# A gated linear attention in front of a two-level mixture of experts: scans with a PSUM operand, scores by row halves, compact state, small first units

## The chip, the cores and the metric

The kernel runs on one core of one Trainium2 chip. The metric is the device time of one execution in microseconds (us). Three runs of the kernel before took 591.95 us in the median (591.56 to 595.39).

## The reference

Two parts follow each other. The attention part has 4 batches, 8 heads, 768 time steps and head size 48; per head it carries a 48 x 48 state:

```
for t in range(S):
    state = alpha[:, :, t, :, None] * state + einsum('bhd,bhe->bhde', k[:, :, t], v[:, :, t])
    y[:, :, t] = einsum('bhd,bhde->bhe', q[:, :, t], state)
```

Its output, 3072 rows of 384, goes through a mixture of 16 experts in 4 groups: each row takes the best group, then the best expert of it, both by the largest logit; its row of the output is `combined * (relu(x @ w1[g, e]) @ w2[g, e])` with w1 of 384 x 1024, w2 of 1024 x 384 and `combined` the product of the two softmax weights. All data is float32.

## The kernel before, in words

**Attention.** The 768 steps of a batch are cut into 6 chunks of 128, so there are 24 chunks, numbered n = 0 to 23, and one turn of the main loop (line 385) per chunk; it is called a step below. Heads are taken in pairs p = 0 to 3: one head of a pair lies on partitions 0 to 47, the other on 64 to 111, so R = 112 partitions are used. Within a chunk the decay is turned into weights on q and k, so that the chunk's inner sum is a masked matrix product, and a state is carried from chunk to chunk.

- `decayed(u, p)` (lines 164 to 191) prepares one pair for a *unit* of 3 chunks (8 units). VectorE (DVE) runs a scan backward over 384 columns (`rev`, line 181), a reciprocal (line 184), a scan forward (`cq`, line 185) and the decay of the whole chunk (`tot`, line 187). GpSimd (POOL) multiplies k by `rev` (`kp`, line 188) and q by `cq` (`qp`, line 189). ScalarE (ACT) copies q into `qb` (line 191), where the two heads of a pair stand in separate columns with zeros between. Both scans multiply by the decay and add a tile (`ends`, `starts`) that lies in SBUF.
- `scores(n)` (line 193): 4 matmuls of 256 columns over all 112 rows into two PSUM banks (line 200); DVE masks each bank (`sm`, line 204).
- `outputs(n)` (line 237): 4 matmuls with the state (line 244), 8 with `v` (line 249), an ACT copy to `yt` (line 253).
- `next_state` (line 210): 4 transposes of `kp` (line 218), ACT copy to `kt` (line 219), 4 matmuls with `v` (line 224); DVE adds (line 230) and multiplies by `tot` (line 232), each once per head of the pair, into a state tile with zeros off the blocks.
- `to_rows` (line 256): 4 matmuls with `wr` (line 265), a DVE sum into logits (line 268), an ACT copy into the rows `x` (line 271).
- Once per batch `choose` (line 274, some two dozen short DVE operations) finds the expert, and `send` (line 330) counts places and writes the rows into `slots_d` in DRAM by indirect DMA from POOL (line 353). The last batch does this in three cuts.

**Experts.** For each of 16 experts the first 224 slots are fetched, transposed, and multiplied by w1 (line 443) and w2 (line 452); DVE scales and POOL scatters the rows of the output (line 457). A loop for slots beyond 224 follows (line 535).

**What sets the order.** Each engine runs its own instructions in order. A scheduler arranges them from the program text and from the buffers: tiles named in a pool rotate through its `bufs`, and an instruction that needs a buffer waits until its last reader is done. Loads of q, k and alpha (`qka`, 5 buffers) and of weights go through SyncE's (SP's) queue, `v` and `xg` through ACT's. The rows `x` of a batch have 2 buffers, so those of batch b wait for the indirect DMAs of batch b - 2 (the first write into them is line 323).

## Time and profile before

| | |
|---|---|
| median of 3 runs | 591.95 us |
| the profiled execution | 591.61 us, its span 589.9 us |
| TensorE busy | 492.1 us (83%) |
| VectorE busy | 225.6 us (38%) |
| GpSimd busy | 138.2 us (23%) |
| ScalarE busy | 105.0 us (18%) |
| DMA | 92.82 MB, mean 157 GB/s |

The span runs from the first to the last instruction; 1.7 us of the execution lie outside it. Busy shares are means over very unlike stages: the attention ends at about 235 us, and the experts take the rest. A step is located here by its matmuls with the state (line 244), which come once per n. [...] Each matmul of float32 appears as two records.

### The profile page before, as it was taken

The numbers are of one execution on the slowest core, as the hardware profiler recorded it, in microseconds if no ns is written. First come the engines' busy times: TensorE is split into PE (matmuls) and PEld (weight loads), VectorE is DVE, ScalarE is ACT, GpSimd is POOL, SyncE is SP. The second block draws the span as 40 slices with busy tenths as digits, with TensorE's granted clock in tenths as the row PEclk, the third lists the DMA queues.
The fourth block names the chain that finished last, engine by engine and source line by source line (L and its number), as shares of the span: only waits on it lengthen the run. The fifth ranks groups of instructions, "written<-read, shape, count | busy, mean of one in ns | idle before, by whom it ended". The sixth has DMA issues, their size and how long they took to land. (4 is left out here: it accounts for less than half of the span.)

```text
span 589.9 us, 6890 instructions
## 1 busy us (share of the span) xinstructions
PE 492.1 (83%) x2588; PEld 389.0 (66%) x2588; DVE 225.6 (38%) x607; ACT 105.0 (18%) x209; POOL 138.2 (23%) x141
## 2 busy tenths in 40 slices
PE   0475896786876798169999999999999999999992
PEld 0363785675765677166886688678767876887681
DVE  7748978768875775821111110111011101110100
ACT  0313333223232422100110111011101100110010
POOL 6506551456065503300011001100110010011001
PEclk9996797898789999559999999999999999999997
DMA  8983479444332002233645464555545554645000
GB/s 274 366 261 107 136 264 314 148 138 122 114 106 82 0 2 82 80 96 121 246 151 202 177 234 163 174 204 204 191 144 220 182 220 137 230 140 213 21 8 24
DMA packets 18674, 92.82 MB, mean 157 GB/s; under 512 B 2693, under 2 KB 6394, under 8 KB 14032
## 3 DMA queue, kind: packets, MB, share of 16 engines
q1 hardware_dynamic: 10512, 72.44, 35.7%
q10 hardware_dynamic: 4800, 10.46, 5.5%
q0 software_dynamic: 3328, 9.47, 4.3%
q8 instruction: 21, 0.34, 0.2%
q14 instruction: 13, 0.11, 0.1%
HBM read 77.36 MB, written 15.78 MB: 158 GB/s over the span
## 5 line engine op out<-in xcount | busy, mean ns | idle before, releaser
L452 PE MATMUL bank<-w,hT 128*96 128x384 f32 (+1 forms) x512 | 168.2, 487 | 0.0
L443 PEld LDWEIGHTS bank<-xt_e,w 128*128 128x128 f32 x768 | 147.6, 193 | 5.8 <-issue 2.4
L443 PE MATMUL bank<-xt_e,w 128*128 128x224 f32 x768 | 151.0, 357 | 0.6 <-DVE xt_e L432 0.6
L452 PEld LDWEIGHTS bank<-w,hT 128*96 128x96 f32 (+1 forms) x512 | 89.2, 177 | 70.1 <-issue 38.3
L457 POOL DMA_INDIRECT out_dram<-yo,dst x32 | 30.4, 950 | 301.2 <-DVE yo L455 274.6
L445 ACT ACTIVATE hT<-bank 128x448 f32<-128x448 f32 x64 | 34.8, 543 | 290.4 <-PE bank L443 290.4
L200 PE MATMUL bank<-qb,kp 112*128 112x256 f32 x192 | 58.4, 453 | 30.7 <-ACT qb L191 29.3
L455 DVE TENSOR_SCALAR yo<-bank,xg 128x384 f32<-128x384 f32 (+1 forms) x32 | 19.7, 615 | 154.1 <-PE bank L452 154.1
L200 PEld LDWEIGHTS bank<-qb,kp 112*128 112x128 f32 x192 | 41.9, 233 | 39.6 <-issue 18.2
L189 POOL TENSOR_TENSOR qp<-qka,cq 112x384 f32<-112x384 f32 x32 | 42.3, 1331 | 50.0 <-PE bank L244 33.0
L188 POOL TENSOR_TENSOR kp<-qka,rev 112x384 f32<-112x384 f32 x32 | 37.3, 1178 | 45.1 <-DVE rev L181 17.3
L224 PE MATMUL bank<-v,kt 128*112 128x96 f32 x160 | 22.9, 292 | 28.3 <-ACT kt L219 28.3
L191 ACT COPY qb<-qp 48x384 f32<-48x384 f32 x64 | 32.6, 510 | 64.6 <-POOL qp L189 63.9
L224 PEld LDWEIGHTS bank<-v,kt 128*112 128x112 f32 x160 | 19.3, 196 | 32.6 <-ACT kt L219 32.6
L485 DVE TENSOR_TENSOR dst<-xg,drop 128x1 int32<-128x1 f32 (+1 forms) x32 | 3.8, 155 | 95.1 <-DMA xg<-slots_d 54.5
L185 DVE TENSOR_TENSOR_SCAN cq<-qka,starts 112x384 f32<-112x384 f32 x32 | 39.7, 1244 | 0.5
L181 DVE TENSOR_TENSOR_SCAN rev<-qka,ends 112x384 f32<-112x384 f32 x32 | 33.7, 1059 | 10.8 <-POOL kp L188 6.4
L244 PE MATMUL bank<-qp,state 112*112 112x128 f32 x192 | 27.6, 291 | 11.6 <-DVE state L232 11.6
L244 PEld LDWEIGHTS bank<-qp,state 112*112 112x112 f32 x192 | 25.8, 191 | 15.7 <-issue 10.8
L204 DVE TENSOR_TENSOR sm<-bank,causal 128x512 f32<-128x512 f32 x48 | 32.0, 680 | 7.3 <-PE bank L200 7.0
L353 POOL DMA_INDIRECT slots_d<-x,place x24 | 23.6, 984 | 46.1 <-ACT yt L253 23.3
L265 PE MATMUL bank<-wr,yt 112*128 112x116 f32 x192 | 31.4, 316 | 0.0
(99 smaller groups left out, 290.2 us busy)
## 6 DMA issues: line engine op xcount, KB each, us to landing
w<-in_w_dram SPq DMA_DIRECT2D x32, 1536.0 KB, 6.8
qka<-in_qka_dram SPq DMA_DIRECT2D x32, 505.8 KB, 4.6
slots_d<-blank SPq DMA_DIRECT2D x1, 5404.0 KB, 28.2
v<-in_v_dram ACTq DMA_DIRECT2D x4, 1152.0 KB, 10.8
xg<-slots_d ACTq DMA_DIRECT2D x16, 193.0 KB, 6.7
xg<-slots_d ACTq DMA_DIRECT2D x16, 144.8 KB, 6.5
out_dram<-yo,dst POOLq DMA_INDIRECT x32, 6.0
slots_d<-x,place POOLq DMA_INDIRECT x24, 2.7
```

Source lines behind the costliest of these rows:

```text
L181: nc.vector.tensor_tensor_scan(out=flat(rev)[:, ::-1], data0=az[:, US:0:-1], data1=flat(ends)[:, ::-1], initial=0.0, op0=ALU.mult, op1=ALU ...
L185: nc.vector.tensor_tensor_scan(out=flat(cq), data0=az[:, 0:US], data1=flat(st), initial=0.0, op0=ALU.mult, op1=ALU.add)
L188: nc.gpsimd.tensor_tensor(out=flat(kp[:, p]), in0=k, in1=flat(rev), op=ALU.mult)
L189: nc.gpsimd.tensor_tensor(out=flat(qp[:, p]), in0=q, in1=flat(cq), op=ALU.mult)
L191: nc.scalar.copy(out=qd[r, p, :, i, :], in_=qp[r, p])
L200: nc.tensor.matmul(z[:, (p - g) * 2 * P:(p - g + 1) * 2 * P], lhsT=kp[:, p, c, :], rhs=qd[:, p, c].rearrange("r h s -> r (h s)"), start=Tr ...
L204: nc.vector.tensor_tensor(out=sm[:, 2 * g:2 * g + 4, :], in0=z.rearrange("p (h i) -> p h i", h=4), in1=causal[:, None, :].to_broadcast([P, ...
L224: nc.tensor.matmul(z[0:R, p * D2:(p + 1) * D2], lhsT=kt[:, p * R:(p + 1) * R], rhs=v[:, bc, p * D2:(p + 1) * D2], start=True, stop=True)
L244: nc.tensor.matmul(z[0:R, p * P:(p + 1) * P], lhsT=st[:, p, :], rhs=qp[:, p, c, :], start=(p == 0), stop=False, skip_group_check=True)
L443: nc.tensor.matmul(z[:, k * n:(k + 1) * n], lhsT=w1[:, dc, f * P:(f + 1) * P], rhs=xt[:, dc, 0:n], start=(dc == 0), stop=(dc == DC - 1))
L445: nc.scalar.activation(out=hT[:, f0:f0 + 2, 0:n], in_=z[:, 0:2 * n].rearrange("p (f t) -> p f t", f=2), func=AF.Relu)
L452: nc.tensor.matmul(zy[0:n, 0:DM], lhsT=hT[:, f, c0:c0 + n], rhs=w2[:, f, :], start=(f == 0), stop=(f == FC - 1))
```

## The change

Only the attention part and its input layout change; the experts' code is the same.

- **Scans.** Their second source lies in PSUM: one bank `starts`, filled with 3e38, with one column of ones. A chunk has 129 columns, the first of them a decay of 3e38; the scans multiply and take the minimum, so that at this column they restart at the second source. The backward scan's first column of each chunk is then the chunk's whole decay, and `tot` goes away. PSUM is left with 7 banks for the rest in place of 8.
- **Scores.** Per pair two matmuls of 128 columns, one over partitions 0 to 47 and one over 64 to 111, each into the bank of its head. `qb` and its ACT copies go away.
- **State.** It is kept compact (112 x 4 x 48); the matmuls with `v` write each head into its own half (8 matmuls of 48 columns), DVE does two adds and one multiply, and ACT copies it into tiles with zeros off the blocks (`blocks`). The transposes come before `outputs`.
- **Order.** Units are 1, 2 and then 7 times 3 chunks (9 units). Decays, `choose` and `send` are cut into portions that a queue `later` hands out at three places of a step. The rows `x` have 3 buffers, the loads 8, each in two DMAs. The blanking of `slots_d`, the weights' loads and the loads of `qka` stand later in a step.

```diff
@@ the pools
-    xp = ctx.enter_context(tc.tile_pool(name="xrows", bufs=2))
+    xp = ctx.enter_context(tc.tile_pool(name="xrows", bufs=3))
-    pp = ctx.enter_context(tc.tile_pool(name="psum", bufs=8, space=PSUM))
+    pp = ctx.enter_context(tc.tile_pool(name="psum", bufs=7, space=PSUM))
...
-        inp = gla.enter_context(tc.tile_pool(name="inp", bufs=5))
+        inp = gla.enter_context(tc.tile_pool(name="inp", bufs=8))
...
+        fix = gla.enter_context(tc.tile_pool(name="fix", bufs=1, space=PSUM))
+        starts = fix.tile([P, 512], F32, name="starts")
+        one_col = starts[0:R, 511:512]
+        nc.vector.memset(starts, HUGE)
+        nc.vector.memset(one_col, 1.0)
...
+        units = [(0, 0, 1), (0, 1, 2), (0, UC, UC)]
+        units += [(b, c, UC) for b in range(1, B) for c in (0, UC)]
@@ decayed
-            nc.vector.tensor_tensor_scan(out=flat(rev)[:, ::-1], data0=az[:, US:0:-1],
-                                         data1=flat(ends)[:, ::-1], initial=0.0,
-                                         op0=ALU.mult, op1=ALU.add)
-            nc.vector.reciprocal(out=st[:, :, 0], in_=rev[:, :, 0])
-            nc.vector.tensor_tensor_scan(out=flat(cq), data0=az[:, 0:US], data1=flat(st),
-                                         initial=0.0, op0=ALU.mult, op1=ALU.add)
-            nc.vector.tensor_tensor(out=tot[:, :, p], in0=rev[:, :, 0], in1=a0, op=ALU.mult)
-            nc.gpsimd.tensor_tensor(out=flat(kp[:, p]), in0=k, in1=flat(rev), op=ALU.mult)
-            nc.gpsimd.tensor_tensor(out=flat(qp[:, p]), in0=q, in1=flat(cq), op=ALU.mult)
-            for i, r in enumerate(heads):
-                nc.scalar.copy(out=qd[r, p, :, i, :], in_=qp[r, p])
+            def back():
+                nc.vector.tensor_tensor_scan(
+                    out=flat(rev)[:, ::-1], data0=a[:, W:0:-1],
+                    data1=one_col.to_broadcast([R, W]), initial=1.0, op0=ALU.mult, op1=ALU.min)
+                nc.gpsimd.tensor_tensor(out=kp, in0=k, in1=rev[:, :, 1:A1], op=ALU.mult)
+
+            def forth():
+                nc.vector.reciprocal(out=st.rearrange("r (c s) -> r c s", s=A1)[:, :, 0],
+                                     in_=rev[:, :, 0])
+                nc.vector.tensor_tensor_scan(out=flat(cq), data0=a[:, 0:W], data1=st, initial=1.0,
+                                             op0=ALU.mult, op1=ALU.min)
+                nc.gpsimd.tensor_tensor(out=qp, in0=q, in1=cq[:, :, 1:A1], op=ALU.mult)
+
+            return [(1.0, back), (1.2, forth)]
@@ scores
+            z = [bank() for _ in heads]
+            for p in range(HP):
+                for i, r in enumerate(heads):
+                    nc.tensor.matmul(z[i][:, p * P:(p + 1) * P], lhsT=kp[r, p, c, :],
+                                     rhs=qp[r, p, c, :], start=True, stop=True)
+            for i in range(2):
+                nc.vector.tensor_tensor(out=sm[:, i], in0=z[i].rearrange("p (h i) -> p h i", h=HP),
+                                        in1=causal[:, None, :].to_broadcast([P, HP, P]),
                                         op=ALU.mult)
...
@@ next_state
+            for p in range(HP):
+                for i, r in enumerate(heads):
+                    h = 2 * p + i
+                    nc.tensor.matmul(z[r, p * D:(p + 1) * D],
+                                     lhsT=kt[:, p * R + r.start:p * R + r.stop],
+                                     rhs=vs[b][:, bc, h * D:(h + 1) * D], start=(p == 0), stop=True,
+                                     skip_group_check=True)
...
+                for r in heads:
+                    nc.vector.tensor_tensor(out=new[r], in0=old[r], in1=add[r], op=ALU.add)
+                nc.vector.tensor_tensor(out=new, in0=new, in1=tot.to_broadcast([R, HP, D]),
+                                        op=ALU.mult)
+            blk = blocks[1 + n % 2]
+            for r in heads:
+                nc.scalar.copy(out=blk[r, :, r], in_=new[r])
@@ the main loop
+            if c == 0 and u + 1 < NU:
+                make(u + 1)
+            if n + 1 < LAST and where[n + 1][1] == 0:
+                spend(1e9)
+            sm_next = scores(n + 1) if n + 1 < LAST else None
+            carry = (n + 1) % NC and n + 1 < LAST
+            kt = turned_keys(n) if carry else None
+            spend(2.0)
+            yt_next = outputs(n, sm, blk)
+            if n + 1 < LAST:
+                blk = next_state(n + 1, kt) if carry else blocks[0]
+            spend(1.2)
+            if yt is not None:
+                send_chosen()
+                rows_and_choice(n - 1, yt)
+            spend(1.2)
```

On TensorE one step in the middle of the program (scores, state matmuls, `v` matmuls, transposes, state update, rows) stands before as:

```order
L200 MATMUL bank<-qb_125,kp 128x256 x4
L244 MATMUL bank<-qp,state_127 112x128 x4
L249 MATMUL bank<-sm,v 48x128 x8
L218 MATMUL bank<-ident,kp 128x112 x4
L224 MATMUL bank<-v,kt 112x96 x4
L265 MATMUL bank<-wr,yt 128x116 x4
```

and now as (line 222 the scores, 237 the transposes, 277 and 282 the outputs, 250 the state update, 298 the rows):

```order
L222 MATMUL bank<-qp,kp 128x128 x8
L237 MATMUL bank<-ident,kp 128x112 x4
L277 MATMUL bank<-qp,blocks_129 112x128 x4
L282 MATMUL bank<-sm,v 48x128 x8
L250 MATMUL bank<-v,kt 48x48 x8
L298 MATMUL bank<-wr,yt 128x116 x4
```

The transposes moved ahead of the outputs, and two groups of four matmuls became groups of eight smaller ones.

On DVE, from the masking of step 15 to that of step 16, before (lines 181 and 185 are the scans, which this listing calls SCALAR_TENSOR_TENSOR, 184 the reciprocal, 187 the chunk's decay, 204 the masking, 230 and 232 the state, 268 the logits, 342 the counting of `send`):

```order
L204 TENSOR_TENSOR sm<-bank,causal 128x512 x2
L181 SCALAR_TENSOR_TENSOR rev<-qka,ends 112x384 x2
L184 RECIPROCAL starts_122<-rev 112x3
L187 TENSOR_TENSOR tot<-rev,qka 112x3
L184 RECIPROCAL starts_123<-rev 112x3
L185 SCALAR_TENSOR_TENSOR cq<-qka,starts_122 112x384
L230 TENSOR_TENSOR state_128<-state_127,bank 48x4x48 x2
L232 TENSOR_TENSOR state_128<-state_128,tot 48x4x48 x2
L342 TENSOR_TENSOR seen<-bank,seen 128x16
L268 TENSOR_REDUCE lg<-bank 128x20
L342 TENSOR_TENSOR seen<-bank,seen 128x16
L204 TENSOR_TENSOR sm<-bank,causal 128x512
```

and now, from the same masking on (lines 201 and 209 are the scans, 207 the reciprocal, 225 the masking, 262 and 263 the state, 301 the logits, 382 the counting of `send`):

```order
L225 TENSOR_TENSOR sm<-bank,causal 128x512 x2
L201 SCALAR_TENSOR_TENSOR rev<-qka,starts 112x387
L207 RECIPROCAL starts<-rev 112x3
L209 SCALAR_TENSOR_TENSOR cq<-qka,starts 112x387
L262 TENSOR_TENSOR state_126<-state_125,bank 48x192 x2
L201 SCALAR_TENSOR_TENSOR rev<-qka,starts 112x387
L263 TENSOR_TENSOR state_126<-state_126,rev 112x192
L301 TENSOR_REDUCE lg<-bank 128x20
L382 TENSOR_TENSOR seen<-bank,seen 128x16
L207 RECIPROCAL starts<-rev 112x3
L382 TENSOR_TENSOR seen<-bank,seen 128x16
L209 SCALAR_TENSOR_TENSOR cq<-qka,starts 112x387
```

The chunk's decay is no longer an operation, the state has one multiply in place of two, and a pair's two scans stand together, with the state between two pairs.

On POOL, before, the six indirect DMAs of a batch stand between the multiplications of one unit:

```order
L188 TENSOR_TENSOR kp<-qka,rev 112x384 x4
L189 TENSOR_TENSOR qp<-qka,cq 112x384 x2
L353 DMA slots_d<-x,place 49152x386 x6
L188 TENSOR_TENSOR kp<-qka,rev 112x384 x3
L189 TENSOR_TENSOR qp<-qka,cq 112x384 x2
```

and now between two units, of which the first is complete:

```order
L204 TENSOR_TENSOR kp<-qka,rev 112x384
L211 TENSOR_TENSOR qp<-qka,cq 112x384
L394 DMA slots_d<-x,place 49152x386 x6
L204 TENSOR_TENSOR kp<-qka,rev 112x384
L211 TENSOR_TENSOR qp<-qka,cq 112x384
```

The six DMAs moved behind the last multiplication of the unit that is needed next.

## Rows read from the trace of the kernel before

**Rows 1.** Timeline, TensorE, line 244: steps 3, 6, 18, 23 (start us, us, what, idle)

```profile
64.86 1.04 PE L244 MATMUL bank<-qp,state 112*112 112x128 f32 x8
...
86.77 1.04 PE L244 MATMUL bank<-qp,state 112*112 112x128 f32 x8
...
197.11 1.04 PE L244 MATMUL bank<-qp,state 112*112 112x128 f32 x8
...
233.05 1.10 PE L244 MATMUL bank<-qp,state 112*112 112x128 f32 x8 [0.78 <-DVE state L232]
```

**Rows 2.** Busy time by stage: us, PE, PEld, DVE, ACT, POOL (instructions), PEclk, DMA, GB/s

```profile
86.77:197.11 110.34, 82.78 (x606) 70.79 (x604) 85.58 (x217) 34.38 (x71) 50.66 (x45) 0.88 0.43 140
197.11:233.05 35.94, 29.01 (x255) 25.34 (x254) 23.57 (x98) 10.69 (x24) 8.86 (x9) 1.00 0.09 34
```

**Rows 3.** Groups by line, DVE, 86.77 to 197.11: busy us, mean ns, idle before

```profile
L185 DVE TENSOR_TENSOR_SCAN cq<-qka,starts 112x384 f32<-112x384 f32 x17 | 22.6, 1331 | 0.4
L181 DVE TENSOR_TENSOR_SCAN rev<-qka,ends 112x384 f32<-112x384 f32 x16 | 17.4, 1096 | 6.5 <-POOL kp L188 6.4
L187 DVE TENSOR_TENSOR tot<-rev,qka 112x3 f32<-112x3 f32 x17 | 7.1, 438 | 0.1
L268 DVE TENSOR_REDUCE lg<-bank 128x20 f32<-128x80 f32 x12 | 2.8, 234 | 0.7 <-PE bank L265 0.5
```

**Rows 4.** Single lines, whole program: ns shortest/median/longest, first and last start

```profile
L185 DVE TENSOR_TENSOR_SCAN cq<-qka,starts x32: 925/952/1757, 11.2 to 197.4; 112x384 f32<-112x384 f32 x32
...
L204 DVE TENSOR_TENSOR sm<-bank,causal x48: 658/681/693, 25.2 to 227.3; 128x512 f32<-128x512 f32 x48
...
L230 DVE TENSOR_TENSOR state<-state,bank x40: 318/352/360, 34.6 to 231.8; 48x192 f32<-48x192 f32 x40
...
L232 DVE TENSOR_TENSOR state<-state,tot x40: 350/354/1046, 35.4 to 232.5; 48x192 f32<-48x192 f32 x40
```

**Rows 5.** Waits, 0 to 240 us: who <- for whom, us in total, times, longest

```profile
ACT qb L191 <- POOL qp L189: 63.9, 20, 11.0
...
PE bank L224 <- ACT kt L219: 28.3, 20, 4.9
...
DVE x L323 <- DMA slots_d<-x,place: 12.0, 2, 6.1
```

**Rows 6.** Timeline, DVE: one pair's reciprocal and scan; first and last operation of `choose`

```profile
71.86 0.15 DVE L184 RECIPROCAL starts<-rev 112x3 f32<-112x3 f32 x1
72.11 0.96 DVE L185 TENSOR_TENSOR_SCAN cq<-qka,starts 112x384 f32<-112x384 f32 x1
...
98.16 0.18 DVE L289 TENSOR_REDUCE gmx<-lg 128x6 f32<-128x24 f32 x1
...
103.70 0.19 DVE L322 RECIPROCAL x<-cw 128x6 f32<-128x6 f32 x1
```

**Rows 7.** Timeline, TensorE and its weight loads: a step without scans, up to 226.74 us

```profile
219.97 1.04 PE L244 MATMUL bank<-qp,state 112*112 112x128 f32 x8
220.93 1.08 PE L249 MATMUL bank<-sm,v 128*48 128x128 f32 x16
...
221.94 0.39 PEld L218 LDWEIGHTS bank<-ident,kp 112*128 112x128 f32 x4 [0.18 <-issue]
...
223.22 1.02 PE L224 MATMUL bank<-v,kt 128*112 128x96 f32 x8 [0.68 <-ACT kt L219]
224.00 0.97 PEld L265 LDWEIGHTS bank<-wr,yt 112*128 112x128 f32 x8
225.00 1.90 PE L200 MATMUL bank<-qb,kp 112*128 112x256 f32 x8
```

**Rows 8.** Timeline, DVE: scans that waited for the second and the fourth tile

```profile
10.06 0.96 DVE L181 TENSOR_TENSOR_SCAN rev<-qka,ends 112x384 f32<-112x384 f32 x1 [1.96 <-DMA qka<-in_qka_dram]
...
18.28 0.96 DVE L181 TENSOR_TENSOR_SCAN rev<-qka,ends 112x384 f32<-112x384 f32 x1 [1.97 <-DMA qka<-in_qka_dram]
```

**Rows 9.** Timeline, TensorE at the lower clock: scores of one step

```profile
61.49 3.54 PE L200 MATMUL bank<-qb,kp 112*128 112x256 f32 x8
```

227 lines of the change are left out of this document (116 added, 111 removed).

## The prediction

> **What bounds the kernel now.** I read first where the matmuls with the state stand in time, since they mark the steps. Step 3 starts at 64.86 us, step 6 at 86.77, step 18 at 197.11 and step 23 at 233.05 [rows 1]. So twelve steps in the middle take 110.34 us, 9.2 each, and the last five 35.9 us, 7.2 each. The rest, from 233.05 to the end of the span at 589.9, is 356.85 us of tail and experts, whose code the change leaves alone.
>
> Then the busy times of the two stretches. In the middle DVE is busy for 85.6 of 110.3 us, TensorE for 82.8 at a granted clock of 0.88 [rows 2]. Neither is full, so the next view is what DVE's time consists of and what it waits for. The scans take 22.6 + 17.4 = 40.0 us, the small product for `tot` 7.1 and the logits 2.8 [rows 3]; 17 reciprocals at 0.15 [rows 6] are 2.6; 24 maskings at 0.68 us are 16.3, and two adds at 0.352 and two multiplies at 0.354 in ten of the twelve steps are 14.1 [rows 4]. `choose` runs from 98.16 to 103.9 with two maskings inside [rows 6], so 4.3 us alone, 8.6 for two batches; `send` has some ten operations of the same size, 4 us for two. DVE also waits 12.0 us for indirect DMAs (the first write into a batch's `x` rows) [rows 5] and 6.5 us for POOL before a backward scan [rows 3]. The sum is 114, against 110.3 (neighbours overlap a little): DVE, with what it waits for in its queue, is the bound of the middle. The last five steps have few scans; there TensorE's own sequence of about 6.8 us, with 0.68 waiting for `kt`, sets the pace [rows 7].
>
> Why the scans are long is read from the spread of single lines. A scan takes 0.925 us at least and 1.757 at most [rows 4]. The multiply of the state, also with two sources in SBUF, goes from 0.350 to 1.046. The maskings and the state's add have one source in PSUM, and keep to 0.658 to 0.693 and 0.318 to 0.360 in 48 and 40 runs, though POOL is at work for nearly half of the middle [rows 2, 4]. So operations with two SBUF sources are held up by POOL's, those with a PSUM source are not.
>
> **The change part by part.**
>
> *Scans.* They get a PSUM source and should stay near their undisturbed 0.95 us (a chunk has 129 columns in place of 128, +1%). No scan with a PSUM source is in the trace. From below its bound is the shortest, 0.92; from above the longest, 1.76 [rows 4]. I take 0.95, since the two kinds of operation with a PSUM source were never slowed. The reciprocal is 0.15 us and the scan behind it starts 0.25 us after it [rows 6]; a pair is 0.95 + 0.03 + 0.25 + 0.95, less 0.08 that neighbours overlap: 2.10 us. For the middle twelve steps, 16 pairs: 33.6 us, where scans, `tot` and reciprocals took 49.7.
> Rows first: the add with a PSUM source has a median of 0.352 us, the multiply of the same shape from SBUF alone 0.354 [rows 4]. [...]
>
> *State on DVE.* Two adds at 0.352 and one multiply at about 0.39 (it can still be held up by POOL): 1.1 us for 1.41; over the middle 10.9 for 14.1. The ACT copies of the blocks are new, two of some 0.35 us per step. They lie behind the multiply on the path to the next state matmuls: after its state update TensorE still has rows, scores and transposes, 2.5 us, while DVE and ACT need 1.1 + 0.3 (logits stand between) + 0.7 + 0.4 for handing over, 2.5. I count 0.25 us of waiting per step.
>
> *DVE's waits.* A third buffer for `x` takes the 12.0 us away. The wait for POOL before backward scans (6.5 us) goes with the order: `rev` is now a tile per unit. On POOL the six indirect DMAs come behind the last multiplication of the next unit; queued behind them is only the unit after that, needed two steps later.
> The DVE bill for the middle is then 33.6 + 16.3 + 10.9 + 2.8 + 8.6 + 4 = 76 us, 6.3 per step.
>
> *TensorE.* A step without scans gives, from start to start: state matmuls 0.96, `v` matmuls 1.01, transposes 0.60, waiting 0.68, state update and rows 1.78, scores 1.74 [rows 7]. The wait goes, because the transposes stand ahead of the outputs, which cover the copy to `kt`. The state update becomes 16 records, as the `v` matmuls are: 1.01 for about 0.87. The scores become 8 matmuls of 128 columns on half the rows. If the two halves of a pair run side by side, they cost what four matmuls of 128 columns over all rows cost, 0.96; if not, twice that, 1.92. I take 1.0, since the 16 records of the `v` matmuls, whose outputs lie in two halves, need 1.01 where four full ones need 0.96 [rows 7]. There are two more changes between whole-array and half-array matmuls per step; 0.18 us stands before the transposes at such a place [rows 7], so 0.36. The sum is 0.96 + 1.01 + 0.60 + 1.92 + 1.0 + 0.36 = 5.85 us.
> The gap in TensorE's stream caused by ACT goes too: ACT waited 63.9 us for POOL at its `qb` copies, with `yt` and `kt` queued behind them, and TensorE waited 28.3 us for `kt` [rows 5].
>
> *Both together.* The portions are not even: per six steps two carry 2 to 2.5 pairs and one most of `choose` (7 to 7.5 us on DVE), the others leave TensorE in front (6.1). Step by step the larger of the two gives 40 us per six, 80 for the middle; I add 5 for handing over and for stretches at the lower clock. Middle: 85 us in place of 110.
>
> *Start.* Unit 0 is one chunk, 0.69 MB in place of 2.07. Before, the second tile (1.04 MB) was there at 10.1 us and the fourth at 18.3 [rows 8], so unit 0 lands before 10 and unit 1 before 18. DVE: unit 0 done at about 9.5; unit 1, four pairs of 258 columns at 1.5, and a masking, at 17; unit 2, four pairs at 2.1 with two maskings and two states, 13 us, at 30; POOL, scores and masking behind it, and step 3 starts at 35, not 64.86. Steps 3 to 6: four pairs, two of them in one step, 20 us. The blanking of `slots_d` moves out of this stretch to about step 5; its bytes are the same, and what is queued behind it on SP, unit 6, is needed only in step 12. If it should delay a unit, that would show at step 9 or 12.
>
> *Sum.* Step 6 at 55, step 18 at 140, five more steps at 6.2 (one heavy): step 23 at 171. Then 356.85 as before: a span of 528. With the 1.7 us outside it 529.6, against 591.6 of the profiled execution. That lies 0.3 us under the median, so 530 against 591.95. PSUM's seven banks cost nothing: a step takes six, and each is read within the step.
>
> **Rivals.**
>
> *Row halves do not run side by side* (chance 0.14). Scores 1.92, TensorE's step 6.8. Steps where DVE has more to do swallow some of it: about 0.6 us over 20 steps and 1 at the start, 543. For it: each score matmul now has its own load of 128 columns, and 8 records of such loads need 0.97 us [rows 7], so 16 would need 1.9 if they can't overlap. [...] No run here shows loads into half the rows.
>
> *DVE's bill alone decides* (0.14). The portions fill the gaps: middle 77, start 32, then 18 and 30: step 23 at 157, 516. For it: `choose` in 4.3 us is mostly waiting for its own last result, which other portions can fill.
>
> *The scan is slow from PSUM* (0.04). All at 1.76: 64 scans' worth of 387 columns times 0.81 are 52 us, 582. Against it stands every operation with a PSUM source in the trace.
>
> *Slower: TensorE stays at 1.2 GHz* (0.04). Every step has waits, and after waits the clock falls: scores took 3.54 us in one step [rows 9] against 1.90 [rows 7], 1.86 times as long. If all steps ran so: 5.85 x 1.86 = 10.9 us, 20 of them 218, step 23 at 253, 611. It decides from 9.9 us per step on, that is if the granted clock were near 0.6 throughout. Against it: with longer waits than are left the middle had 0.88, and the last five steps 1.00 [rows 2].
>
> **How the numbers follow.** The forecast, 530, has a chance of 0.62, and 0.02 is left for what I don't see. The range goes from 508, a little under the second rival, to 560: that holds the first rival and 17 us of loads that come late or of lower clock, and leaves out the last two. A measurement of this kernel tells about 1% (6 us) from no change: faster by more 0.93 (all but the last two rivals, and half of the third), within 1% 0.03, slower 0.04.
>
> **What would show it.** Right: forward and backward scans of 0.92 to 1.0 us with a longest below 1.1; no DVE wait for indirect DMA; scores of 8 matmuls in about 1.0 us; step 3 at about 35 us, step 6 at 55, step 18 at 140 and step 23 at 171, and 357 us behind it. Wrong: scans that still reach 1.7 us (POOL holds them all the same); scores of 1.9; step 3 after 45 us (loads); a granted clock under 0.8 between steps 6 and 18; or a tail longer than 360 us, which I took as unchanged.

## The result and the profile after

The kernel after takes 517.41 us in the median of 4 runs (517.22 to 518.40), the kernel before, run beside it, 591.75. The ratio is 0.8735, with a 95% interval of 0.8699 to 0.8770. The forecast was 530 with a range of 508 to 560: the time lies in the range, 12.6 us under the forecast. The profiled execution is one of 517.22 us with a span of 515.5; it is the one read here.

First the steps. This is TensorE's timeline, with the matmuls with the state (line 277 now) of steps 3, 6, 18 and 23. The columns are start in us, duration of the group, engine, line, what, and idle time before it with its releaser:

```profile
42.31 1.13 PE L277 MATMUL bank<-qp,blocks 112*112 112x128 f32 x8
...
58.14 1.04 PE L277 MATMUL bank<-qp,blocks 112*112 112x128 f32 x8
...
132.34 0.93 PE L277 MATMUL bank<-qp,blocks 112*112 112x128 f32 x7
...
161.48 0.69 PE L277 MATMUL bank<-qp,blocks 112*112 112x128 f32 x4 [1.65 <-ACT blocks L267]
```

Set against [rows 1], the 74.4 us of span that went are: 22.6 up to step 3 (64.86 to 42.31), 6.1 in steps 3 to 6, 36.1 in the middle twelve (110.34 to 74.20), 6.8 in steps 18 to 23, and 2.8 in the tail (356.85 to 354.0).

Busy time by stage, the view of [rows 2] (us, then TensorE, its weight loads, DVE, ACT and POOL with their numbers of instructions, TensorE's granted clock as a share of full speed, DMA share, GB/s):

```profile
42.31:58.14 15.83, 14.48 (x185) 12.87 (x185) 14.88 (x28) 5.18 (x11) 8.25 (x9) 1.00 0.60 191
58.14:132.34 74.20, 64.39 (x782) 56.46 (x781) 66.36 (x187) 25.09 (x58) 41.11 (x44) 0.95 0.86 291
132.34:161.48 29.14, 25.98 (x327) 23.04 (x325) 24.94 (x101) 11.97 (x30) 10.43 (x11) 0.94 0.10 36
```

In the middle DVE is now busy for 89% and TensorE for 87%, where it was 78 and 75%. Nearly all of TensorE's idle 9.8 us there are waits of one kind, shown below. POOL has nearly the same number of instructions there (44 for 45) and needs 41.1 us for them in place of 50.7.

The groups of DVE in the middle, the view of [rows 3] (count, busy us, mean ns, idle time before):

```profile
L209 DVE TENSOR_TENSOR_SCAN cq<-qka,starts 112x387 f32<-112x387 f32 x17 | 16.3, 958 | 1.3
L225 DVE TENSOR_TENSOR sm<-bank,causal 128x512 f32<-128x512 f32 x24 | 15.2, 677 | 0.0
L201 DVE TENSOR_TENSOR_SCAN rev<-qka,starts 112x387 f32<-112x387 f32 x16 | 15.2, 947 | 0.1
L262 DVE TENSOR_TENSOR state<-state,bank 48x192 f32<-48x192 f32 x16 | 5.5, 346 | 5.1 <-issue 4.9
```

The forward scan has gone from a mean of 1331 ns to 958 and the backward one from 1096 to 947 [rows 3]. The spread shows it better. This is the view of a single line over the whole program (shortest/median/longest ns), to be set beside the 925/952/1757 of [rows 4]; the shortest belongs to the first units, which are narrower:

```profile
L209 DVE TENSOR_TENSOR_SCAN cq<-qka,starts x36: 424/959/961, 4.9 to 136.9; 112x387 f32<-112x387 f32 x28, 112x129 f32<-112x129 f32 x4, 112x258 f32<-112x258 f32 x4
```

The DVE wait of 12.0 us for the indirect DMAs and TensorE's 28.3 for `kt` [rows 5] are gone. What TensorE waits for in the middle is `blocks`. This is the view of the waits there (who <- for whom, us in total, times, longest):

```profile
PE bank L277 <- ACT blocks L267: 9.3, 7, 2.2
```

Last, a step without scans, to be compared with [rows 7]:

```profile
150.98 1.04 PE L277 MATMUL bank<-qp,blocks 112*112 112x128 f32 x8
151.95 1.08 PE L282 MATMUL bank<-sm,v 128*48 128x128 f32 x16
152.86 0.53 PE L250 MATMUL bank<-v,kt 128*48 128x48 f32 x16
153.32 1.15 PE L298 MATMUL bank<-wr,yt 112*128 112x116 f32 x8
154.40 1.16 PE L222 MATMUL bank<-qp,kp 48*128 48x128 f32 x16
155.49 0.60 PE L237 MATMUL bank<-ident,kp 112*128 112x112 f32 x4
155.93 1.04 PE L277 MATMUL bank<-qp,blocks 112*112 112x128 f32 x8
```

It takes 4.95 us from start to start (150.98 to 155.93) and has no gap. The scores (line 222) take 1.09 us of it where they took 1.74, and the state update (line 250) 0.46.

### The profile page after: what moved, and what is told of

Read it like the earlier page. It is cut to its first block, busy times and chain, and to the rows that moved or that the text cites. A ratio compares the mean times of both kernels' runs of the same rounds, so it can differ in the third digit from the quotient of the medians.

```text
span 515.5 us, 7601 instructions
## 1 busy us (share of the span) xinstructions
PE 461.6 (90%) x2940; PEld 365.9 (71%) x2940; DVE 188.1 (36%) x564; ACT 87.6 (17%) x185; POOL 115.8 (22%) x146
## 5 line engine op out<-in xcount | busy, mean ns | idle before, releaser
L525 DVE TENSOR_SCALAR yo<-bank,xg 128x384 f32<-128x384 f32 (+1 forms) x32 | 19.7, 615 | 154.1 <-PE bank L522 154.1
L222 PE MATMUL bank<-qp,kp 48*128 48x128 f32 x384 | 34.1, 306 | 13.9 <-POOL qp L211 13.6
L277 PE MATMUL bank<-qp,blocks 112*112 112x128 f32 x192 | 29.8, 302 | 14.5 <-ACT blocks L267 14.4
L222 PEld LDWEIGHTS bank<-qp,kp 48*128 48x128 f32 x384 | 26.5, 198 | 19.6 <-POOL qp L211 15.6
L204 POOL TENSOR_TENSOR kp<-qka,rev 112x384 f32<-112x384 f32 (+2 forms) x36 | 30.7, 853 | 42.1 <-DVE starts L207 18.1
L277 PEld LDWEIGHTS bank<-qp,blocks 112*112 112x112 f32 x192 | 25.0, 194 | 18.0 <-ACT blocks L267 17.4
L211 POOL TENSOR_TENSOR qp<-qka,cq 112x384 f32<-112x384 f32 (+2 forms) x36 | 29.7, 825 | 17.4 <-DVE cq L209 14.5
L201 DVE TENSOR_TENSOR_SCAN rev<-qka,starts 112x387 f32<-112x387 f32 (+2 forms) x36 | 30.7, 853 | 4.6 <-DMA qka<-in_al_dram 4.5
L209 DVE TENSOR_TENSOR_SCAN cq<-qka,starts 112x387 f32<-112x387 f32 (+2 forms) x36 | 31.3, 869 | 2.9
L282 PE MATMUL bank<-sm,v 128*48 128x128 f32 x384 | 31.1, 304 | 0.0
L394 POOL DMA_INDIRECT slots_d<-x,place x24 | 23.6, 983 | 30.3 <-ACT yt L286 15.3
L298 PEld LDWEIGHTS bank<-wr,yt 112*128 112x128 f32 x192 | 25.6, 208 | 2.0 <-issue 0.9
## 6 DMA issues: line engine op xcount, KB each, us to landing
slots_d<-blank SPq DMA_DIRECT2D x1, 5404.0 KB, 23.4
```

The source lines that it names most:

```text
L201: nc.vector.tensor_tensor_scan(out=flat(rev)[:, ::-1], data0=a[:, W:0:-1], data1=one_col.to_broadcast([R, W]), initial=1.0, op0=ALU.mult, ...
L204: nc.gpsimd.tensor_tensor(out=kp, in0=k, in1=rev[:, :, 1:A1], op=ALU.mult)
L209: nc.vector.tensor_tensor_scan(out=flat(cq), data0=a[:, 0:W], data1=st, initial=1.0, op0=ALU.mult, op1=ALU.min)
L222: nc.tensor.matmul(z[i][:, p * P:(p + 1) * P], lhsT=kp[r, p, c, :], rhs=qp[r, p, c, :], start=True, stop=True)
L277: nc.tensor.matmul(z[0:R, p * P:(p + 1) * P], lhsT=blk[:, p, :], rhs=qp[:, p, c, :], start=(p == 0), stop=False, skip_group_check=True)
L282: nc.tensor.matmul(z[r, p * P:(p + 1) * P], lhsT=vs[b][:, bc, h * D:(h + 1) * D], rhs=sm[:, i, p, :], start=False, stop=True, skip_group_c ...
```

## The experiments

**How they are read.** Eleven kernels were run in three groups, each group beside the kernel before, which took 596.95, 596.72 and 598.17 us there; last came a control, beside 593.13. Ratios are therefore used, not times. The second thing to know is a stall, which is told of at the end of this section: it is in all eight variants of the kernel after in the three groups, and neither in the kernel after itself nor in the control. It falls into the stretches of steps 9 to 12, 15 to 18 and 21 to 23. So the spans were cut at the starts of steps, and the table holds, for each kernel, the time up to step 3, then the stretches between the steps named, then the rest, in us from the profiled execution:

| kernel | to 3 | 3-6 | 6-9 | 9-12 | 12-15 | 15-18 | 18-21 | 21-23 | rest | span |
|---|---|---|---|---|---|---|---|---|---|---|
| before | 64.9 | 21.9 | 31.2 | 24.4 | 30.3 | 24.5 | 22.9 | 13.1 | 356.8 | 589.9 |
| after | 42.3 | 15.8 | 21.0 | 16.0 | 21.6 | 15.5 | 18.6 | 10.5 | 354.0 | 515.5 |
| f0_same_order | 42.2 | 15.8 | 21.0 | 16.1 | 22.2 | 16.1 | 18.6 | 10.5 | 353.2 | 515.7 |
| f9_v_late | 39.3 | 15.8 | 21.4 | 23.6 | 18.7 | 23.1 | 17.0 | 13.8 | 355.4 | 528.0 |
| f10_state_first | 44.0 | 15.4 | 18.3 | 20.5 | 20.5 | 20.1 | 17.9 | 14.1 | 354.9 | 525.6 |
| f1_scan_sbuf_same_order | 45.2 | 18.1 | 25.2 | 24.9 | 22.2 | 23.0 | 19.3 | 13.8 | 354.8 | 546.6 |
| e1_scan_sbuf | 51.2 | 14.5 | 28.0 | 23.2 | 24.2 | 23.4 | 20.5 | 13.7 | 353.8 | 552.4 |
| e5_x2 | 41.4 | 15.8 | 21.0 | 28.5 | 23.5 | 23.8 | 16.3 | 13.8 | 355.0 | 539.0 |
| e6_units3 | 42.2 | 15.8 | 21.3 | 22.5 | 18.6 | 23.4 | 17.1 | 13.9 | 355.3 | 530.2 |
| e7_at_once | 45.0 | 15.8 | 19.9 | 23.8 | 20.7 | 23.5 | 18.0 | 15.4 | 352.7 | 534.9 |
| e8_turn_late | 44.6 | 17.9 | 24.3 | 24.2 | 21.8 | 22.3 | 23.6 | 17.3 | 354.5 | 550.4 |
| e3_rows | 58.3 | 26.2 | 27.9 | 25.8 | 26.3 | 24.9 | 20.5 | 16.9 | 357.0 | 583.8 |
| e4_scan_psum | 60.7 | 19.7 | 25.2 | 24.8 | 22.1 | 22.7 | 24.6 | 15.6 | 356.3 | 571.7 |
| f4_scan_psum_old_order | 60.7 | 21.1 | 27.7 | 24.2 | 23.9 | 24.1 | 21.5 | 15.9 | 356.2 | 575.1 |

The kernel f9_v_late has the order of the kernel after in everything but one load, and has the stall. From step 3 to the end it needs 488.7 us (528.0 less 39.3) where the control needs 473.5. It serves below as the yardstick with the stall in it. This takes the stall to cost the same 15 us in every kernel, which no run shows; prices read against it are estimates.

The three variants of the kernel before (the last three rows) have something like it too. In f4_scan_psum_old_order, which has the order of the kernel before, ACT's copy to `yt` in step 22 starts 2.3 us after ACT is free and 2.9 us after the matmuls that it reads, and no engine of the core is shown to hold it; in the kernel before ACT goes on to it at once. Steps 21 to 23 take 16.9, 15.6 and 15.9 us in these three where the kernel before takes 13.1.

### Scans with both sources in SBUF: e1_scan_sbuf, f1_scan_sbuf_same_order

```diff
-        starts = fix.tile([P, 512], F32, name="starts")
+        starts = buf.tile([P, 512], F32, name="starts")
```

> The kernel after, with the tile `starts` (the scans' second source) in SBUF in place of PSUM; nothing else. Theory (operations of DVE with two SBUF sources are held up by GpSimd's): the scans of 387 columns reach 1.6 to 1.8 us at the longest and 1.1 to 1.3 in the mean, as in the kernel before; by its means (1.33 forward, 1.10 backward against 0.96 and 0.945) 64 scans lose 17 us of DVE, of which 8 to 17 reach the end: 525 to 535. Rival (the gain comes from the order of the work, the scans were long for another reason): longest scan under 1.1 us, 517 plus or minus 3.

Measured: 554.78 us, ratio 0.9303 (0.9279 to 0.9327). The scans had means of 1286 and 1110 ns and a longest of 1709, so the contention came back as the theory says; but 33 us were lost (0.0568 of 592), twice the 8 to 17 that were expected. The scheduler had also put the instructions in another order, so the run could not tell the scans' part from the order's. The second kernel takes the order away as a cause. A table of indices, read off the built program of the kernel after, ties each instruction to the one that stood before it on its engine:

```diff
+        for name, runs in order.items():
+            mine = [i for i in traced if str(i.engine) == "EngineType." + name]
...
+            for j, k in zip(at, at[1:]):
+                tc.add_manual_dep(mine[k], mine[j].name,
+                                  mybir.DependencyInfo(mybir.DependencyClass.NoSync,
+                                                       mybir.DependencyReason.DATA), reason="order")
```

> The scans' second source in SBUF again (as in e1_scan_sbuf), but every engine's order of instructions is fixed to that of the kernel after by edges from a table, so that nothing differs but where `starts` lies. Theory (longer scans, and what is queued behind them): the scans get 1.1 to 1.3 us in the mean and POOL's multiplies 1.1 to 1.3; 56 long scans lose 14 us together, DVE is busy for nine tenths of the middle, so 10 to 17 us reach the end: 527 to 535 on a chip where the kernel after takes 517 (ratio to the kernel before 0.890 to 0.904). Rival (the loss in e1_scan_sbuf was the longer scans alone): 0.930 again. Second rival (it was the order alone): 0.874.

Measured: 547.95 us, ratio 0.9191 (0.9142 to 0.9240). The groups of DVE and then of POOL in this kernel, up to 240 us:

```profile
L209 DVE TENSOR_TENSOR_SCAN cq<-qka,starts 112x387 f32<-112x387 f32 x28 | 37.2, 1329 | 2.3
...
L201 DVE TENSOR_TENSOR_SCAN rev<-qka,starts 112x387 f32<-112x387 f32 x28 | 30.1, 1077 | 0.1
```

```profile
L211 POOL TENSOR_TENSOR qp<-qka,cq 112x384 f32<-112x384 f32 x28 | 31.4, 1123 | 20.2 <-DVE cq L209 15.0 <-PE bank L282 1.9 <-DVE seen L382 1.8
L204 POOL TENSOR_TENSOR kp<-qka,rev 112x384 f32<-112x384 f32 x28 | 30.7, 1096 | 44.0 <-DVE starts L207 26.1 <-DVE rev L201 15.3 <-DVE seen L382 2.6
```

The same groups of POOL in the kernel after:

```profile
L204 POOL TENSOR_TENSOR kp<-qka,rev 112x384 f32<-112x384 f32 x28 | 26.2, 937 | 34.7 <-DVE starts L207 18.1 <-DVE rev L201 13.8 <-DVE seen L382 2.6
L211 POOL TENSOR_TENSOR qp<-qka,cq 112x384 f32<-112x384 f32 x28 | 25.5, 911 | 15.0 <-DVE cq L209 12.1 <-DVE seen L382 1.3 <-DVE sm L225 0.8
```

Both sides pay: 56 scans lose 14.1 us together (28 times 371 and 133 ns, against means of 958 and 944 over the 28 of the kernel after), and 56 multiplies of POOL 10.4. Scans of 0.96 us stretch to 1.65, multiplies of 0.91 to 1.62, and in the kernel after, with one source in PSUM, neither goes over 1.0. What it is in SBUF that the two engines contend for was not shown. The ratio lies outside the theory's range and the rivals': 27 us over the kernel after. If the stall is set aside by the yardstick, 15.6 us are the edit's: 2.9 more up to step 3, and 501.4 from there on against 488.7. That is the theory's 10 to 17. The rest of the 27 is put down to the stall.

### The same in the kernel before: e4_scan_psum, f4_scan_psum_old_order

```diff
-    pp = ctx.enter_context(tc.tile_pool(name="psum", bufs=8, space=PSUM))
+    pp = ctx.enter_context(tc.tile_pool(name="psum", bufs=6, space=PSUM))
...
-        ends = buf.tile([R, UC, P], F32, name="ends")
...
+        ends = fix.tile([P, 4, P], F32, name="ends")[0:R, 0:UC, :]
...
-        starts = [buf.tile([R, UC, P], F32, name=f"starts{i}") for i in range(2)]
+        starts = [fix.tile([P, 4, P], F32, name="starts")[0:R, 0:UC, :]]
```

> The kernel before, with both tiles that its scans add (`ends`, and `starts` as one tile) in PSUM, which leaves 6 banks for the rest; nothing else. Theory (contention with GpSimd): forward and backward scans 0.92 to 1.0 us with no long ones; DVE is the bound of the middle, so the middle twelve steps lose 8 us and the whole 10 to 17: 575 to 582. Rival (in the old order DVE's saved time turns into waits for GpSimd, TensorE and the indirect DMAs): 588 to 592.

Measured: 575.71 us, ratio 0.9659 (0.9591 to 0.9726), 20 us and more than the 10 to 17 of the theory. The scans have means of 946 and 939 ns and a longest of 955. With the order of the kernel before held by the table, and both `starts` in PSUM:

> The kernel before, every engine's order fixed to its own by edges from a table, with the second sources of both scans (`ends`, and both `starts`) in PSUM; 5 banks are left in place of 8. Theory (contention): 32 forward scans shrink from 1.24 to 0.95 us in the mean and 32 backward from 1.06 to 0.94, 13 us, `tot` by 6; with TensorE's shorter waits and higher clock 12 to 25 us reach the end: ratio 0.958 to 0.98. Rival (in the old order the waits for GpSimd, `kt` and the indirect DMAs swallow it): 0.99 to 1.00. Second rival (five banks are too few): over 1.00.

Measured: 578.72 us, ratio 0.9705 (0.9644 to 0.9765), 17.6 us, the middle of the theory's 12 to 25. Its scans up to 240 us:

```profile
L182 DVE TENSOR_TENSOR_SCAN rev<-qka,ends 112x384 f32<-112x384 f32 x32 | 30.2, 944 | 12.7 <-POOL kp L189 6.4 <-DMA qka<-in_qka_dram 6.2
L186 DVE TENSOR_TENSOR_SCAN cq<-qka,starts 112x384 f32<-112x384 f32 x32 | 29.9, 940 | 0.6
```

So moving one operand brings 17 to 20 us in the old order too; five banks in place of eight did not eat it.

### Scores by row halves alone: e3_rows

```diff
-            for i, r in enumerate(heads):
-                nc.scalar.copy(out=qd[r, p, :, i, :], in_=qp[r, p])
...
+                for i, r in enumerate(heads):
+                    nc.tensor.matmul(z[i][:, p * P:(p + 1) * P], lhsT=kp[r, p, c, :],
+                                     rhs=qp[r, p, c, :], start=True, stop=True)
```

> The kernel before, with the scores by row halves alone (`qb` and its ACT copies gone). First question, TensorE: if the two halves of a pair run side by side, a step's 8 score matmuls take 1.0 to 1.2 us, otherwise about 1.9; before 1.74. Second question, the end: if ACT's wait for GpSimd with `kt` and `yt` queued behind it was what held the middle, the 28 us that TensorE waited for `kt` come back: about 563; if DVE with its scans and waits is the bound, only the steps without scans gain (0.6 to 1.3 us each, some 8 of them): 580 to 587.

Measured: 585.79 us, ratio 0.9831 (0.9804 to 0.9859), 10 us. TensorE's timeline in a step without scans:

```profile
207.74 1.11 PE L258 MATMUL bank<-wr,yt 112*128 112x116 f32 x8
208.78 1.16 PE L195 MATMUL bank<-qp,kp 48*128 48x128 f32 x16
209.88 1.13 PE L237 MATMUL bank<-qp,state 112*112 112x128 f32 x8
```

Sixteen records in 1.10 us up to the next group, where eight records of 128 columns over all rows took 0.96 [rows 7]: the halves do run side by side. For the end the second answer's number held, but not where it put the gain, the steps without scans. In the table all of the profiled gain lies before step 3 (6.5 us); from there to the end the two kernels need 525.0 and 525.5. Step 22 of e3_rows takes 10.6 us for 6.3, with a stall of 1.6 us before ACT's copy to `yt` in it. The first answer was not tested cleanly, since most of TensorE's wait for `kt` stayed, 18.2 us up to 240 where it was 28.3 [rows 5]:

```profile
PE bank L217 <- ACT kt L212: 18.2, 18, 4.4
```

### Two buffers for the rows: e5_x2

```diff
-    xp = ctx.enter_context(tc.tile_pool(name="xrows", bufs=3))
+    xp = ctx.enter_context(tc.tile_pool(name="xrows", bufs=2))
```

> The kernel after, with two buffers in place of three for the rows `x`. Theory (the wait of DVE for the indirect DMAs belongs to the second buffer): DVE waits again before the first write into `x` of batches 2 and 3, 12 us in the kernel before, and these come to the end nearly whole: 525 to 530. Rival (in the new order the rows are sent early enough): under 2 us of such waits, 517 to 519.

Measured: 538.54 us, ratio 0.9027 (0.9010 to 0.9045). DVE's waits between 57 and 184 us in this kernel:

```profile
DVE state L262 <- issue: 13.7, 2, 7.2
DVE x L360 <- DMA slots_d<-x,place: 10.6, 1, 10.6
```

The time is above both ranges. The second row is the theory's wait, once in place of twice. It stands in steps 9 to 12, which take 28.5 us, 4.8 over the yardstick; from step 3 to the end it is 8.9 us over it. So the third buffer is worth about 9 us, by the yardstick. The first row is the stall.

### Small first units undone: e6_units3

```diff
-        units = [(0, 0, 1), (0, 1, 2), (0, UC, UC)]
-        units += [(b, c, UC) for b in range(1, B) for c in (0, UC)]
+        units = [(b, c, UC) for b in range(B) for c in (0, UC)]
```

> The kernel after with eight units of three chunks; the small first units are undone (two units are loaded ahead). Theory (the first matmuls wait for four pairs of a whole unit and its 2 MB): step 0 starts at about 25 us in place of 18.5, step 3, which needs unit 1, at 46 to 50 in place of 42.3, and the rest as it was: 521 to 526 (ratio 0.880 to 0.889). Rival (the loads bound the start: by step 3 both have brought the same bytes, and both made eight pairs): step 3 at 41 to 44, 515 to 519 (0.870 to 0.877).

Measured: 531.67 us, ratio 0.8920 (0.8865 to 0.8976), outside both. The stretches tell why. Step 0 starts at 24.16 us in place of 18.55, as the theory has it; but step 3 starts at 42.2 in both kernels and step 6 at 58.1, as the rival has it; and from step 3 on the kernel needs 488.0, the yardstick 488.7. So its loss is the stall, and the small first units bring nothing: the first matmuls come 5.6 us sooner and wait that much longer for the next unit.

### All portions at once: e7_at_once

```diff
-            while later and us > 0:
+            while later:
```

> The kernel after with the queue `later` emptied wherever it is asked: a unit's eight scans, and all of `choose` or `send`, stand in one place of a step. Theory (the portions keep the state's and the masking's short operations from waiting behind scans): one step in three has 8 us of scans ahead of its state on DVE, TensorE waits 2 to 4 us more there; six such units: 530 to 540 (ratio 0.895 to 0.913). Rival (the scheduler spreads them anyway, since it orders by what is ready): 516 to 521 (0.871 to 0.880).

Measured: 537.35 us, ratio 0.9017 (0.8969 to 0.9064). The number is the theory's, its reason is not: from step 3 on the kernel needs 489.9 us, 1.1 over the yardstick. Step 3 comes 2.7 us later. Set against the yardstick the portions are worth some 4 us, so the scheduler spreads most of the work by itself.

### Transposes behind the outputs: e8_turn_late

```diff
-            kt = turned_keys(n) if carry else None
             spend(2.0)
             yt_next = outputs(n, sm, blk)
+            kt = turned_keys(n) if carry else None
```

> The kernel after with the transposes written behind the outputs, where the kernel before had them. Theory (TensorE waits 0.68 us for `kt` in every step in which it sets the pace, as before): 20 steps, some 8 to 20 of them bound by TensorE: 522 to 531 (ratio 0.882 to 0.897). Rival (DVE sets the pace of most steps and TensorE has room): 517 to 519 (0.873 to 0.877).

Measured: 555.78 us, ratio 0.9319 (0.9220 to 0.9419), the largest loss of all and far beyond the theory's 522 to 531. From step 3 on it is 17.1 us over the yardstick, up to step 3 2.3 over the kernel after. TensorE's waits from step 6 to step 23:

```profile
PE bank L250 <- ACT kt L238: 15.5, 14, 3.5
PE bank L277 <- ACT blocks L267: 6.4, 6, 3.0
```

The 14 waits for `kt` are 1.1 us each, not the 0.68 of [rows 7]. In the kernel after TensorE is idle for 0.3 us before these matmuls in the whole middle. How much of the 19 us is the place of the transposes and how much the order that the scheduler made of it was not separated.

### The load of the second `v` later: f9_v_late

In ACT's row of the table one entry, 11, the second load of `v`, moves from the third place to behind the third copy to `yt`:

```diff
-0-1 11 2-7 10 8-9 12-13 16 14-15 17-18 21 19-20 22-27 41 28-33 38 34 40 35 39 36-37 42-48 51 49-50 52-57 71
+0-7 10 8-9 12-13 11 16 14-15 17-18 21 19-20 22-27 41 28-33 38 34 40 35 39 36-37 42-48 51 49-50 52-57 71 58-63
```

> The kernel after with every engine's order fixed to its own, but for one instruction: the load of the second batch's `v` (1.15 MB, issued at 1.3 us, used from step 6 on) stands on ACT's queue behind the third copy to `yt`, at some 36 us. Theory (the first units' loads share the DMA engines with it): at 260 to 310 GB/s it takes 4 us of them; step 3 at 38 to 40 us in place of 42.3, the rest as it was: 513 to 515 (ratio 0.866 to 0.870 where the kernel after has 0.8735). Rival (DVE, busy for 10.4 of 11 us from 25 to 36 us, sets the pace there): step 3 at 42, 517.

Measured: 529.82 us, ratio 0.8870 (0.8822 to 0.8918). The theory's mechanism is there: step 3 starts at 39.3 us, 3.0 sooner, and step 9 is still 2.7 sooner. DVE's second wait for alpha at the start, 1.90 us in the kernel after, is gone, and unit 1 is done at 18.5 us in place of 20.5. So loads did hold the start. The expectation had one thing wrong: the load goes out at 7.7 us in the kernel after, not at 1.3. The time is over both ranges: the stall took more than the 3 us back.

### The state first: f10_state_first

In the table DVE's entries for the state move ahead of up to 14 others, and the multiply directly behind the adds; on ACT the copies to `blocks` move ahead of the copy to `x` in 8 steps. One of the 13 places in DVE's order, in step 8:

```diff
-L201 SCALAR_TENSOR_TENSOR rev<-qka,starts 112x387
-L207 RECIPROCAL starts<-rev 112x3
-L209 SCALAR_TENSOR_TENSOR cq<-qka,starts 112x387
-L262 TENSOR_TENSOR state_126<-state_125,bank 48x192 x2
-L201 SCALAR_TENSOR_TENSOR rev<-qka,starts 112x387
-L263 TENSOR_TENSOR state_126<-state_126,rev 112x192
+L262 TENSOR_TENSOR state_126<-state_125,bank 48x192 x2
+L263 TENSOR_TENSOR state_126<-state_126,rev 112x192
+L201 SCALAR_TENSOR_TENSOR rev<-qka,starts 112x387
+L207 RECIPROCAL starts<-rev 112x3
+L209 SCALAR_TENSOR_TENSOR cq<-qka,starts 112x387
+L201 SCALAR_TENSOR_TENSOR rev<-qka,starts 112x387
```

> The kernel after with every engine's order fixed to its own, but for the state: in 13 of 20 steps DVE's adds and multiply are moved ahead of the scans, maskings and parts of `choose` that ran between the end of the matmuls with `v` and them (0.45 to 2.7 us), the multiply always directly behind the adds, and in 8 steps ACT copies the blocks ahead of the rows `x`. Theory (TensorE waits for `blocks` and comes back at the lower clock): its 9.3 us of such waits in the middle mostly go, and 3 to 6 us of slow matmuls with them; what DVE does is the same: 500 to 509 (ratio 0.845 to 0.86). Rival (DVE's bill decides; what was passed over, scans and masking, is late in its place): 514 to 520 (0.868 to 0.878).

Measured: 528.93 us, ratio 0.8880 (0.8828 to 0.8932). From step 3 on it needs 481.6 us, 7.1 less than the yardstick, but step 3 comes 1.7 us later than in the kernel after. TensorE still waits for `blocks` 7.1 us between steps 6 and 18, where it was 9.3: what was passed over is late in its place, the rival's reason. The time is over both ranges; with the yardstick's 15 us of stall set aside it lies between the two. A kernel with both of the last two edits was not run.

### The control: f0_same_order

The table alone, with the kernel after's own order.

> The control for the kernels with a fixed order: the kernel after with its own order fixed by the table and nothing else changed; every engine's instructions are the same as the kernel after's, one for one. It also gives the base on the chips of the experiments, where the kernel before takes 596 to 599 us in place of 591.75. First theory (a stall of some 7 us in steps 10 and 16, where DVE's add of the state waits for nothing that the profile shows while GpSimd issues six indirect DMAs, comes with what the experiments changed): no such stall, step 10 to 11 and step 16 to 17 in 4.6 us each, ratio 0.873. Rival (the stall depends on the chip or the run, not on the edits): steps 10 to 11 and 16 to 17 take 7 to 10 us, the waits at the add sum to 10 to 14 us, ratio 0.885 to 0.895, and the small losses of e6_units3, f9_v_late and f10_state_first are this stall and not their edits.

Measured: 519.21 us (6 runs, 515.27 to 521.74), ratio 0.8750 (0.8715 to 0.8784), the kernel after's. So the table costs nothing. Steps 10 to 11 and 16 to 17 take 4.6 us each, and there is no stall. **The stall** is best seen by setting TensorE's timeline in step 10 of the kernel after against that of f9_v_late. First the kernel after:

```profile
87.92 0.53 PE L250 MATMUL bank<-v,kt 128*48 128x48 f32 x16
88.38 1.15 PE L298 MATMUL bank<-wr,yt 112*128 112x116 f32 x8
89.45 1.16 PE L222 MATMUL bank<-qp,kp 48*128 48x128 f32 x16
```

Then f9_v_late, TensorE and behind it DVE:

```profile
85.17 0.82 PE L250 MATMUL bank<-v,kt 128*48 128x48 f32 x16
85.93 1.29 PE L298 MATMUL bank<-wr,yt 112*128 112x116 f32 x8
87.27 0.38 PE L222 MATMUL bank<-qp,kp 48*128 48x128 f32 x2
88.01 0.50 PE L222 MATMUL bank<-qp,kp 48*128 48x128 f32 x5 [0.36 <-issue]
89.45 0.50 PE L222 MATMUL bank<-qp,kp 48*128 48x128 f32 x4 [0.95 <-issue]
```

```profile
91.05 0.73 DVE L262 TENSOR_TENSOR state<-state,bank 48x192 f32<-48x192 f32 x2 [7.02 <-issue]
```

But for the one load, the instructions and their order are the same. In the one the scores run through in 1.16 us, in the other they come in handfuls, with gaps in which TensorE waits for nothing that the profile shows, and DVE's add starts 5 us after the matmuls that it needs. POOL issues six indirect DMAs meanwhile, at the same 1.28 us apart in both, and the DMA share is 1.03 in both stretches. f9_v_late and f10_state_first ran on the same chip as the control, so it isn't the chip. The first theory gave the control's numbers, but it is not shown: eight unlike edits have the same stall, and something besides the edits differed too, since on this chip the kernel before took 598.17 us in the group with the stall and 593.13 beside the control. Whether the edits or the conditions of those groups bring the stall is open.

## Why the prediction was right, and where it was not

What the runs give to each part, of 74 us in all: the scans' operand 15 to 20, the transposes ahead of the outputs up to 19, the row halves with the ACT copies 10 (in the kernel before), the third buffer 9, the portions 4, the small first units nothing. These don't add up to a sum, since each was taken from a different whole, and the lower end of the scans' and those of the third buffer, the transposes and the portions hang on the yardstick; the compact state was not tried alone.

**Scans: right.** 0.95 us was taken; 0.944 and 0.958 were measured, and none over 0.961. The reason, contention with POOL, is shown from both sides by f1_scan_sbuf_same_order (means of 1077 and 1329 ns with both sources in SBUF) and f4_scan_psum_old_order (944 and 940 with one in PSUM). Of the two bounds the lower was the right one, and a source in PSUM adds no time that shows: these means of 940 and 944 ns are of scans of 384 columns, for which the forward scan's median with both sources in SBUF is 952 [rows 4].

**DVE's bill of 76 us for the middle: right as a sum, wrong as a time.** The 42 groups of DVE in the middle add up to 76.1 us. But the engine is busy for 66.4 us in all: the 187 instructions overlap at their ends by 9.7, some 50 ns each. The bill took this off for scan pairs alone. The kernel before showed it already: the durations in the prediction's first list, without the 18.5 us of waits, are 95.5 us, and DVE's busy time there is 85.58 [rows 2]; the prediction called this a little. The other term, 9 us for uneven steps, handing over and lower clock, was well sized: DVE is idle for 7.8 of the 74.2 us. So the step that failed is "middle: 85 us": the missed overlap makes up nearly all of the 10.8 that it was too long. The rival "DVE's bill alone decides" gave 516, the nearest figure, by luck: its start, 32 us, was 10.3 too early, and its other stretches were 2.2, 2.8 and 0.9 too long, with 2.8 in the tail. In the middle its 77 is nearer than 85, but DVE is not full there, and that portions fill the gaps of `choose` is not shown; e7_at_once gives them some 4 us in all.

**TensorE's floor of 5.85 us per step: too high.** 4.95 was measured. The state update is 0.46 us where 1.01 was taken (its 16 records are 48 columns wide, and they too lie in two halves), transposes 0.44 for 0.60, the `v` matmuls 0.91 for 1.01. The 0.36 for two more changes between whole and half array does not show at all, since the step has no gap. Rows are 1.08 for 0.91, and scores, at 1.09 for 1.0, were near. Since DVE has more to do in most steps, little hung on it in the middle; in steps 18 to 23 it made 29.1 us of 31.

**Row halves side by side: right.** 1.09 us, and 1.10 alone in e3_rows, where 1.0 was taken and 1.92 was the rival. The rival took 16 loads to need 1.9 us, since 8 loads of all rows need 0.97 [rows 7]; in the step shown above, 16 loads of half the rows need 0.97 as well:

```profile
154.40 0.97 PEld L222 LDWEIGHTS bank<-qp,kp 48*128 48x128 f32 x16
```

**DVE's waits: right in the cause.** They are gone, and e5_x2 brings one of 10.6 us back. The gain, by the yardstick, is nearer to 9 us than to 12.

**Waiting for `blocks`, 0.25 us a step: too low.** It is 9.3 us in twelve steps, 0.78 a step, in 7 places of up to 2.2 us. At the places where it is long, scans, maskings or parts of `choose` stand ahead of the state in DVE's queue. That they are the whole cause is not shown: f10_state_first moved the state past them, and 7.1 us of waits were left.

**Start: step 3 at 35 us was too early.** It came at 42.3. The step that failed first is the times at which units 0 and 1 are done on DVE, 9.5 and 17 us: they were 11.1 and 20.5, which is 3.5 of the 7.3 us. Unit 2 then took 14.0 us where 13 was counted, and step 3 came 7.8 us behind it where 5 was counted; these two were not taken apart. DVE waited for alpha twice, and this is its timeline:

```profile
7.90 0.42 DVE L201 TENSOR_TENSOR_SCAN rev<-qka,starts 112x129 f32<-112x129 f32 x1 [2.61 <-DMA qka<-in_al_dram]
...
14.56 0.69 DVE L201 TENSOR_TENSOR_SCAN rev<-qka,starts 112x258 f32<-112x258 f32 x1 [1.90 <-DMA qka<-in_al_dram]
```

The estimate counted the bytes of the units and left out those beside them: loads of `v` go out at 1.3 and 7.7 us, and the DMA share is 1.02 from 5 to 10 us and 1.01 from 10 to 15. f9_v_late shows that the second costs 3.0 us at step 3, and that the wait at 14.56 us is its doing; what the first costs no run shows. And the small units, to which the prediction gave the whole gain of the start, bring nothing by step 3 (e6_units3). Why the start is 22 us shorter all the same was not taken apart; in the kernel before, the scans alone brought 4 us of it (e4_scan_psum) and the row halves 6.5 (e3_rows).

**Steps 3 to 6 and the tail.** 15.8 us for 20: with the clock at 1.00 the steps ran at 4.6 to 6.5; the blanking is issued at 51.93 us, still within this stretch, and no operation of an engine waits for a DMA there. The tail is 354.0 for 356.85.

**The lower clock: not the rule.** The frequency in the last rival's name is shown by no run: the traces give the granted clock as a share of full speed. It was 0.95 in the middle, where that rival asked for about 0.6.

Together: 7.3 later to step 3, then 4.2, 10.8, 1.9 and 2.8 sooner: 12.4 us under the span of 528. That the time came out so near is in part luck: the start's miss hid more than half of the middle's.

## What to carry to other kernels

Where DVE and GpSimd work at the same time, look at the spread of single lines: the forward scan took between 0.925 and 1.757 us here [rows 4], and one operand moved to PSUM ended this on both engines (in the kernel after no scan over 0.961 us, no multiply over 0.996; 15 to 20 us in all). Add up durations for a full engine, but divide by what its busy time says: neighbours overlap, here by an eighth. And when a scheduler orders the work, hold the order fixed before an edit's price is read, and run the unedited order as a control in the same way; two of the edits here seemed to cost 11 and 17 us and, by the yardstick, cost 0 and 4.
